# A fourth block product by a second Strassen level in the second layer, two more units done so, and a new order of VectorE's additions

## The chip, the cores and the metric

The kernel runs on one core of a Trainium2 chip, as one launch. The core's engines each work through a queue of their own in order: TensorE (PE in the profile, with its weight loads as PEld), VectorE (DVE), ScalarE (ACT) and GpSimd (POOL). SyncE (SP) issues most of the DMAs; GpSimd issues those that add what they carry to their destination. TensorE writes to PSUM, which has eight banks of 128 partitions by 512 float32 elements here; VectorE or ScalarE must read a bank before it is written anew. The metric is the time of one execution in microseconds (us), as the device reports it.

## What is computed

```python
# q, k, v: (4, 8, 768, 64); w_in: (512, 2048); w_out: (2048, 512); all float32
for t in range(S):                        # retention: a recurrent state per batch and head
    state = gamma * state + einsum('bhd,bhe->bhde', k[:, :, t], v[:, :, t])
    y[:, :, t] = scale * einsum('bhd,bhde->bhe', q[:, :, t], state)
x = y.transpose(0, 2, 1, 3).reshape(B * S, H * D)     # (3072, 512)
h = x @ w_in
out = maximum(0.01 * h, h) @ w_out                    # leaky ReLU between two layers
```

## The kernel before

The 768 time steps are cut into six chunks of 128 steps, each with 512 tokens (4 batches). The 2048 hidden columns are cut into four units of 512. For a chunk and a unit the first layer is a 512 x 512 product with 512 tokens, then the leaky ReLU, then the second layer, whose result is added to the chunk's output `o` (four blocks of 128 x 2 x 256, 2048 elements per partition). Both are done by the Winograd form of Strassen's algorithm: seven block products M1 to M7 instead of eight, on sums and differences of the blocks.

Chunks 0 and 1 are worked in a first part that the change does not touch in its behaviour. Chunks 2 to 5 are worked in the loop at L1445: 16 steps n = 0 to 15, with chunk c = 2 + n // 4 and unit u = n % 4. A step does the second layer of (c, u), while the first layer of the following step n + 1 is done in two groups between its parts:

- `inner_steps` (L1339) is the first layer, by two Strassen levels: the outer products' operands are split again, so that a matmul is 128 x 128 by 128 columns. Group 0 has four of the outer products (28 matmuls, each of two instructions), group 1 the other three (21 matmuls). They use banks 0 to 3. Of the seven inner products, ScalarE copies the results of five out of PSUM, and VectorE adds the last two (M3 once, M7 twice, L1362 to L1365) to what is there. Bank 1 is free after VectorE's M3 addition.
- `outer` (L1374) adds the inner results to the hidden blocks `g`, two additions after group 0 and five after group 1, and gives ScalarE the leaky ReLU of each.
- `differences` (L629) makes the four operands that the second layer needs beside `g`. VectorE does it at the start of a step, ahead of the evacuation of group 0.
- `output` (L741) is the second layer as seven whole products of eight matmul instructions (128 x 128 by 256 columns) each. Steps 0 to 3 and step 15 use it.
- Steps 4 to 14 use `trunk` (L1290) instead: M1, M5, M6 and later M7 as whole products in banks A = 5, C = 7, B = 4, and the remaining three products by a second level in `leaf_steps` (L1255), which are seven inner products of three matmuls each, in banks 6, 7, 2 and 5. Their moving sums are made by GpSimd (`leaf_sums`, L1242, four operations of 384 elements). Their weights are kept in DRAM (`leaf_kept`), written once per unit in steps 0 to 3 from sums that VectorE makes (`sums_of_rows`), and loaded again for every step (`load_rows`, three DMAs of 448 KB).
- `trunk_taken` (L1321) adds banks A and C to `o`, in a chunk's first unit by copies of ScalarE. M6's bank is added inside `trunk`. `leaf_results_taken` (L1279) adds the leaf results to `o`: after units 0 to 2 by a DMA with `accum_op=add` that GpSimd issues, after unit 3 by VectorE, three additions of 512 elements, each stored to the output.
- `sums_of_x` makes the second-level sums of the next chunk's x: in unit 2 those of group 0, in unit 3 those of group 1, which are wanted by group 1 of the same step.
- In units 0 and 1 of chunks 2 to 4 a step also has a *visit* (`joint_visit`, L414) between group 0 and `trunk`: the retention of two batches of the next chunk, in banks 0, 7, 1 and 2. Its first 16 instructions write banks 0 and 7, the next ones bank 1 and 2. VectorE reads all four at L468. Behind the trunk's products follow the scores of the next two batches (`scores_of_pair`, L358) with their masks and state sums on VectorE.

The order of all instructions is the order in which the program writes them; the schedule is manual, and waits come only from data and from buffers in use. In a step by leaves without a visit, before, VectorE has: four differences, three evacuations of group 0, two additions of `outer`, the sums of x where there are some, then M6's addition to `o`, then A's and C's, three evacuations of group 1, five additions of `outer`, M7's addition, three evacuations of the leaves.

All additions of the kernel stand at one line each in the profile, since they go through helpers: L612 (`plus`) and L615 (`minus`).

Of the kernel before, what the change touches and what calls it, by code (L numbers as in the profile page):

```python
# [22 lines left out]
def kernel(  # L23
# [334 lines left out]
    def scores_of_pair(c, b, banks=None, mid=None):  # L358
# [28 lines left out]
        for j in range(2):  # L387
            am = work.tile([128, 2, HP // 2, 2, C // 2], FP32, tag=f"am{j}", name=f"am{j}_{c}_{b}")
            nc.vector.tensor_tensor(
                out=am.rearrange("p b m i t -> p (b m i) t"),  # L390
                in0=at[j].rearrange("p b m i t -> p (b m i) t"),
                in1=mask[:, 0].unsqueeze(1).to_broadcast([128, 2 * HP, C // 2]), op=ALU.mult)
            weights.append(am)
# [7 lines left out]
        if not last:  # L401
            state_of[p] = halves_of_states.pop(0)
            plus(state_of[p], mid, sums[1])
        mid_of[p] = old, mid
# [206 lines left out]
    def plus(out, a, b):  # L611
        nc.vector.tensor_tensor(out=out, in0=a, in1=b, op=ALU.add)  # L612

    def minus(out, a, b):
        nc.vector.tensor_tensor(out=out, in0=a, in1=b, op=ALU.subtract)  # L615
# [13 lines left out]
    def differences(x, t, last=True):  # L629

        minus(t[:, 0], x[:, 1], x[:, 0])
        minus(t[:, 1], x[:, 3], t[:, 0])
        minus(t[:, 2], x[:, 2], t[:, 1])
        if last:
            last_difference(x)

    def last_difference(x):
        minus(x[:, 1], x[:, 3], x[:, 1])
# [169 lines left out]
    last_three = {}  # L808
# [9 lines left out]
    def new_g(c, u):  # L818
# [3 lines left out]
        last_three[c, u] = both[:, 2:5]  # L822
# [361 lines left out]
    leaf_kept = [dram.tile([128, 3, 7, C], FP32, name=f"leaf_kept_{u}") for u in range(NU)]  # L1184
# [3 lines left out]

    def leaf_rooms():

        free = [flat_of(unit(k)[:, 2:5]) for k in (1, 3, 5)]
        spare = [x2_place[0][:, 21 * C :], streamed_flat[0][:, 21 * C :]]
        more = [spare[i // 2][:, ds(i % 2 * 3 * C, 3 * C)] for i in range(4)]
        return free, spare, [x.rearrange("p (q n) -> p q n", q=3) for x in more]

    def rows_of(u):

        if u < NU - 1:
            return [((0, 3, 1), unit(2 * u + 1)[:, 2:5])]
        return [((0, 3, 2), units[2 * u + 1][1]), ((1, 2, 1), last_s4)]  # L1200

    def sums_of_rows(u):

        free, _, more = leaf_rooms()
        if u == NU - 1:
            more = more[0:2] + [x[:, 7 * C : 10 * C].rearrange("p (q n) -> p q n", q=3)
                                for x in free[0:2]]
        bases = []
        for at, blocks in rows_of(u):
            which = slice(*at)  # L1210
            a11, a21, a12, a22 = (blocks[:, :, k, ts(m, C)] for k in range(2) for m in range(2))
            r = [x[:, which] for x in more]
            plus(r[0], a21, a22)
            minus(r[1], r[0], a11)
            minus(r[2], a12, r[1])
            minus(r[3], a11, a21)
            bases.append((which, blocks))

        def keep():
            for which, blocks in bases:  # L1220
# [4 lines left out]
            for j, r in enumerate(more):  # L1225
                nc.sync.dma_start(out=leaf_kept[u][:, :, 3 + j], in_=r)
        return keep

    def load_rows(n):

        free, spare, _ = leaf_rooms()
        leaf_weights[:] = [x[:, 0 : 7 * C].rearrange("p (j n) -> p j n", j=7)
                           for x in (free[0], free[1], spare[1])]
        for to, kept_rows in zip(leaf_weights, (leaf_kept[at_of(n)[1]][:, i] for i in range(3))):
            nc.sync.dma_start(out=to, in_=kept_rows)

    leaf_weights = []

    def by_leaves(n):
        return n >= NU and n < N2 - 1  # L1240

    def leaf_sums(n):  # L1242

        free, spare, _ = leaf_rooms()
        made = [x.rearrange("p (q n) -> p q n", q=3)
                for x in (free[0][:, 7 * C : 10 * C], free[1][:, 7 * C : 10 * C],
                          spare[0][:, 0 : 3 * C])]
        three = last_three[at_of(n)]
        b11, b12, b21, b22 = (three[:, :, k, ts(h, C)] for k in range(2) for h in range(2))
        for out, a, b in ((made[0], b12, b11), (made[1], b22, made[0]), (made[2], b21, made[1]),  # L1250
                          (b12, b22, b12)):
            nc.gpsimd.tensor_tensor(out=out, in0=a, in1=b, op=ALU.subtract)
        return [b11, b21, *made, b22, b12]

    def leaf_steps(n, moving):  # L1255

        ps = [bank[i][:, 0 : 3 * C].rearrange("p (i n) -> p i n", i=3) for i in (6, 7, 2, 5)]
        results = leaf_results()
        for m, q, j, s in INNER:
            for i in range(3):  # L1260
                nc.tensor.matmul(ps[q][:, i], lhsT=leaf_weights[i][:, j], rhs=moving[s][:, i],  # L1261
# [14 lines left out]
    def leaf_results():  # L1276
        return flat_of(unit(5)[:, 2:5]).rearrange("p (i q n) -> p i q n", i=3, q=4)

    def leaf_results_taken(c, o, final):  # L1279

        results = leaf_results()
        if not final:
# [7 lines left out]
    def trunk(c, o, part, first, final):  # L1290
# [3 lines left out]
        for m, x, sa, rhs, start in (("M1", "A", 0, g[:, 0], True), ("M5", "C", 4, gd[:, 0], True),  # L1294
# [14 lines left out]
            elif m == "M7":  # L1309
# [7 lines left out]
                if final:  # L1317
                    nc.sync.dma_start(out=out[c, 3], in_=o[:, 3])
# [292 lines left out]
```

## Time and profile before

| | us |
|---|---|
| three runs | 633.33, 634.01, 635.36 (median 634.01) |
| the profiled execution, whole | 633.81 |
| its span, first to last instruction | 632.1 |
| busy in the span: TensorE, weight loads | 624.7, 570.5 |
| VectorE, ScalarE, GpSimd | 498.1, 283.5, 81.4 |
| step 6 (chunk 3, unit 2), start to start of the next | 22.54 |
| DMA with addition into `o`, issue to landing, median of nine | 9.2 |

The granted clock of TensorE is 1.000 over the span. The page's busy times are sums over an engine's instructions; the chain that ended last is followed back from the last instruction, at each step to what released it. Timelines list an engine's instructions in order of time: start, length, engine, line, operation, output and input, how many, and in brackets how long the engine had been idle and what released it. Where one line stands for several instructions, the length is that of all of them.

Steps start where group 0 of the next step's first layer starts on TensorE: step 2 at 305.15 us, step 3 at 328.18, step 4 at 351.21, step 5 at 378.19, step 6 at 405.25, step 7 at 427.79, step 8 at 450.33, step 9 at 477.32, step 13 at 571.01, step 14 at 593.55, step 15 at 616.09.

### The profile page before, as it was taken

How to read it: one execution, taken by the hardware profiler on the slowest of the kernel's cores; microseconds unless marked ns; L12 is line 12 of the kernel's file. 1: busy time of each engine (PE TensorE's matmuls, PEld its weight loads, DVE VectorE, ACT ScalarE, POOL GpSimd, SP SyncE). 2: the span in 40 equal slices, each digit the busy share in tenths (PEclk: the TensorE clock that was granted, in tenths of full speed). 3: DMA queues.
4: the chain of work that ended last, by engine and by line, in shares of the span. 5: the costliest groups of instructions: out<-in, count | busy, mean ns of one | idle time of the engine just before them, and what ended most of it. 6: DMA issues, size and time to landing. Idle time of an engine off the chain costs nothing.

```text
span 632.1 us, 15063 instructions
## 1 busy us (share of the span) xinstructions
PE 624.7 (99%) x6284; PEld 570.5 (90%) x6284; DVE 498.1 (79%) x803; ACT 283.5 (45%) x559; POOL 81.4 (13%) x98
## 2 busy tenths in 40 slices
PE   8999999999999999999999999999999999999997
PEld 5888888888888889899999999999998999999996
DVE  5679769889979976668887768799848889866765
ACT  5876646347443114352442452634434424544540
POOL 2000000000011010101000033313033023033200
PEclk9999999999999999999999999999999999999999
DMA  8941325547772998295964888998479579689724
GB/s 330 404 138 34 133 67 208 163 145 226 260 276 81 334 350 289 89 347 168 340 209 157 280 293 250 342 293 260 157 240 306 159 230 278 206 263 271 192 45 116
DMA packets 103219, 141.18 MB, mean 223 GB/s; under 512 B 4328, under 2 KB 82024, under 8 KB 103152
## 3 DMA queue, kind: packets, MB, share of 16 engines
q1 hardware_dynamic: 101552, 132.53, 63.3%
q0 software_dynamic: 1296, 7.08, 5.6%
q8 instruction: 49, 0.80, 0.5%
q10 hardware_dynamic: 304, 0.62, 0.3%
q14 instruction: 18, 0.15, 0.1%
HBM read 108.49 MB, written 24.64 MB: 211 GB/s over the span
## 4 chain that ended last, share of the span: by engine, by line
PE 90%; DMA 5%; ACT 2%; DVE 2%; issue 0%; SPq 0%; DVEq 0%; ACTq 0%
PE bank L1348 26%; PE bank L1299 12%; PE bank L668 11%; PE bank L1261 8%; PE C_h L668 4%; PE B_o L668 4%; PE A_h L668 4%; PE A_o L668 4%; PE C_o L668 4%; PE B_h L668 4%; PE D_o L668 2%; PE D_h L668 2%; DMA x_words<-in_weights_dram 1%; DMA wa<-kept 1%; DMA in<-in_kv_dram 1%; PE bank L371 1%
## 5 line engine op out<-in xcount | busy, mean ns | idle before, releaser
L612 DVE TENSOR_TENSOR made<-made,bank 128x512 f32<-128x512 f32 (+1 forms) x96 | 56.1, 617 | 39.9 <-PE bank L1348 35.9
L1348 PEld LDWEIGHTS bank<-x,wb 128*128 128x128 f32 x672 | 77.6, 192 | 1.1 <-ACT bank L1352 0.3
L1348 PE MATMUL bank<-x,wb 128*128 128x128 f32 x672 | 77.9, 275 | 0.1
L612 DVE TENSOR_TENSOR o<-o,bank 128x512 f32<-128x512 f32 (+3 forms) x75 | 55.2, 767 | 24.3 <-ACT bank L782 6.2
L615 DVE TENSOR_TENSOR g<-g 128x512 f32<-128x512 f32 x96 | 64.1, 688 | 5.3 <-ACT g L1390 0.6
L1348 PE MATMUL bank<-x,wa 128*128 128x128 f32 x512 | 67.6, 275 | 0.0
L1299 PE MATMUL bank<-g,w 128*128 128x256 f32 x288 | 66.1, 382 | 0.7 <-DVE x L468 0.7
L1348 PEld LDWEIGHTS bank<-x,wa 128*128 128x128 f32 x512 | 62.8, 192 | 0.3
L1299 PEld LDWEIGHTS bank<-g,w 128*128 128x128 f32 x288 | 53.2, 190 | 8.0 <-DVE x L468 1.1
L1348 PE MATMUL bank<-t,wa 128*128 128x128 f32 x384 | 53.4, 275 | 0.1
L1348 PEld LDWEIGHTS bank<-t,wa 128*128 128x128 f32 x384 | 48.0, 192 | 0.3 <-DMA wa<-kept 0.3
L612 DVE TENSOR_TENSOR g<-made 128x512 f32<-128x512 f32 x64 | 44.0, 709 | 3.0
L1352 ACT COPY bank<-bank 128x512 f32<-128x512 f32 (+1 forms) x32 | 16.6, 520 | 60.1 <-PE bank L1348 59.8
L1390 ACT ACTIVATE g<-g 128x512 f32<-128x512 f32 x64 | 38.5, 631 | 8.2 <-DVE g L612 8.2
L668 PE MATMUL bank<-g,w 128*128 128x256 f32 x168 | 38.0, 382 | 0.0
L668 PEld LDWEIGHTS bank<-g,w 128*128 128x128 f32 x168 | 31.3, 190 | 4.2
L668 PE MATMUL bank<-g,last 128*128 128x256 f32 (+1 forms) x148 | 32.6, 375 | 0.0
L668 PEld LDWEIGHTS bank<-g,last 128*128 128x128 f32 x148 | 27.0, 190 | 3.9 <-DVE g L615 0.4
L1261 PE MATMUL bank<-g,w 128*128 128x128 f32 x176 | 26.8, 275 | 0.0
L668 PE MATMUL A_h<-x,w 128*128 128x256 f32 x112 | 26.6, 380 | 0.0
L1303 ACT COPY bank<-bank 128x512 f32<-128x512 f32 x11 | 6.3, 570 | 41.1 <-PE bank L1299 41.1
L1283 POOL DMA_DIRECT2D o<-w x9 | 8.1, 903 | 125.2 <-DVE g L615 65.6
(255 smaller groups left out, 1234.8 us busy)
## 6 DMA issues: line engine op xcount, KB each, us to landing
wa<-kept SPq DMA_DIRECT2D x16, 1344.0 KB, 9.4
raw<-in_weights_dram SPq DMA_DIRECT2D x31, 512.0 KB, 4.4
wb<-kept SPq DMA_DIRECT2D x16, 896.0 KB, 5.5
w<-leaf_kept SPq DMA_DIRECT2D x22, 448.0 KB, 4.6
wa<-kept SPq DMA_DIRECT2D x16, 448.0 KB, 6.1
wb<-kept SPq DMA_DIRECT2D x16, 448.0 KB, 6.3
o<-w POOLq DMA_DIRECT2D x9, 768.0 KB, 9.2
out_dram<-o SPq DMA_DIRECT2D x23, 256.0 KB, 2.5
```

Source lines behind the costliest of these rows:

```text
L371: nc.tensor.matmul(at[j][ts(h, 64), n, m, i], lhsT=x[ts(j, 64), 1, a, ts(h, 64)], rhs=x[ts(j, 64), 0, a, ts(h, 64)], start=(n == 0 and a = ...
L612: nc.vector.tensor_tensor(out=out, in0=a, in1=b, op=ALU.add)
L615: nc.vector.tensor_tensor(out=out, in0=a, in1=b, op=ALU.subtract)
L668: nc.tensor.matmul(to, lhsT=block(w, sa)[:, k, ts(i, 128)], rhs=rhs[:, k, a:z], start=(first and (i == 0 or split) and n == 0 and k == 0), ...
L1261: nc.tensor.matmul(ps[q][:, i], lhsT=leaf_weights[i][:, j], rhs=moving[s][:, i], start=(i == 0 and m in ("M1", "M5", "M4")), stop=True, sk ...
L1283: nc.gpsimd.dma_start(out=o[:, 0:3].rearrange("p i k n -> p (i k n)"), in_=results.rearrange("p i q n -> p (i q n)"), accum_op=ALU.add)
L1299: nc.tensor.matmul(ps[x][:, i, :], lhsT=block(2 * u + 1, sa)[:, k, ts(i, 128)], rhs=rhs[:, k, :], start=(start and i == 0 and k == 0), sto ...
L1303: nc.scalar.copy(out=ps["B"], in_=ps["A"])
L1348: nc.tensor.matmul(ps[q][:, i], lhsT=w[:, j, i], rhs=part_of(moving[i], s), start=(i == 0 and m in ("M1", "M5", "M4")), stop=True, skip_gr ...
L1352: nc.scalar.copy(out=ps[3], in_=ps[0])
L1390: nc.scalar.activation(g[:, i], g[:, i], AF.Prelu, alpha=0.01)
```

## The change

The fourth product, M7, goes into the leaves as well: `trunk` keeps M1, M5 and M6, and `leaf_steps` does seven inner products of four matmuls. Steps 2 and 3 are done by `trunk` and leaves too, with weights that stay on the chip: their sums are made by GpSimd (four operations of 512 elements in step 1, twelve smaller ones in step 3). VectorE's weight sums for units 0 and 1 are eight operations each (four of 128 and four of 384 elements) instead of four.

After the leaves VectorE adds the result of M7 to another one (512 elements); then the 2048 results go to `o` by the accumulating DMA after units 0 to 2, and by one addition of VectorE at a chunk's end and in step 14. The stores of the output follow that.

In steps without a visit, A's addition stands right behind M1, C's behind M5 with `outer`'s two additions after it, and M6's behind M6, except in unit 2, where it is behind `outer`'s five. In visiting steps the visit with its loads stands ahead of `outer`'s two additions, and GpSimd's leaf sums in step 9 wait for the differences of x. In visiting steps by leaves the scores use banks 1, 6, 2 and 3, and the second mask comes behind the state sums. In step 14 the differences for step 15 stand ahead of the last three inner products of the leaves. The diff, cut to its core:

```diff
     def scores_of_pair(c, b, banks=None, mid=None, second_mask_last=False):
...
+        masks(range(1 if second_mask_last else 2))
...
+        if second_mask_last:
+            masks((1,))
...
+    ON_CHIP = range(2, NU)
...
     def by_leaves(n):
-        return n >= NU and n < N2 - 1
+        return ON_CHIP[0] <= n < N2 - 1
...
     def load_rows(n):
-        for to, kept_rows in zip(leaf_weights, (leaf_kept[at_of(n)[1]][:, i] for i in range(3))):
-            nc.sync.dma_start(out=to, in_=kept_rows)
+        for i in range(4):
+            to = free[(1, 3)[i // 2]][:, ds(i % 2 * 7 * C, 7 * C)]
+            to = to.rearrange("p (j n) -> p j n", j=7)
+            nc.sync.dma_start(out=to, in_=leaf_kept[at_of(n)[1]][:, i])
...
     def leaf_steps(n, moving):
-            for i in range(3):
-                nc.tensor.matmul(ps[q][:, i], lhsT=leaf_weights[i][:, j], rhs=moving[s][:, i],
+            for i, to in enumerate(TARGETS):
+                nc.tensor.matmul(ps[q][:, to], lhsT=leaf_weights[i][j], rhs=moving[s][:, i],
...
-    def leaf_results_taken(c, o, final):
-        results = leaf_results()
-        if not final:
-            nc.gpsimd.dma_start(out=o[:, 0:3].rearrange("p i k n -> p (i k n)"),
-                                in_=results.rearrange("p i q n -> p (i q n)"), accum_op=ALU.add)
-            return
-        for i in range(3):
-            plus(o[:, i], o[:, i], results[:, i].rearrange("p (k h) n -> p k (h n)", k=2))
-            nc.sync.dma_start(out=out[c, i], in_=o[:, i])
+    def leaf_results_taken(n, o, by_dma):
+        results = leaf_results(n)
+        plus(results[:, 2], results[:, 2], results[:, 3])
+        flat = results.rearrange("p i q n -> p (i q n)")
+        o = o.rearrange("p i k n -> p (i k n)")
+        if by_dma:
+            nc.gpsimd.dma_start(out=o, in_=flat, accum_op=ALU.add)
+        else:
+            plus(o, o, flat)
...
+    def trunk_taken(o, first, part):
+        def to(n):
+            return room[part].unsqueeze(1).to_broadcast([128, n, 2, N])
+        if part == "A":
+            if first:
+                nc.scalar.copy(out=o[:, 0], in_=room["A"])
+            else:
+                plus(o[:, 0], o[:, 0], room["A"])
+        elif part == "C":
...
+                plus(o[:, 1:4:2], o[:, 1:4:2], to(2))
...
+        else:
+            plus(o[:, 1:4], o[:, 1:4], to(3))
...
         if visiting:
+            if u == 0:
+                xs[c + 1] = new_x(c + 1)
             joint_visit(c + 1, 2 * u)
-            if by_leaves(n):
+            if leaves:
                 load_rows(n)
+            outer(n + 1, 0)
+            if u == 1:
+                behind = differences(*xs[c + 1])
...
+        if leaves and not visiting:
+            products(steps, 1)
+            trunk_taken(os[c], u == 0, "A")
+            if more and u == NU - 1:
+                sums_of_x(c + 1, 1)
+            products(steps, 1)
+            trunk_taken(os[c], u == 0, "C")
+            outer(n + 1, 0)
+            if c + 1 < NC and u == 2:
+                sums_of_x(c + 1, 0)
+            products(steps, 1)
+            if u != 2:
+                trunk_taken(os[c], u == 0, "B")
         else:
-            products(steps, 1)
+            products(steps, 3)
...
+            if scores_next and leaves:
+                scores_of_pair(*scores_next, [bank[i] for i in (1, 6, 2, 3)],
+                               second_mask_last=True)
...
+        if n in (0, 1):
+            keep.append(sums_of_rows(n))
+        if n in (1, 3):
+            keep.append(sums_of_rows({1: 2, 3: 3}[n], nc.gpsimd))
...
+            if leaves and not visiting and u == 2:
+                trunk_taken(os[c], False, "B")
+        if leaves:
+            leaf = leaf_steps(n, moving)
+            last_one = n + 2 == N2
+            for count, ready in ((1, 1), (1, 1), (2, 2)) if last_one else ((4, 3), (1, 1)):
+                products(leaf, count)
                 for _ in range(ready):
                     later.pop(0)()
-            products(leaves, 8)
-            leaf_results_taken(c, os[c], u == NU - 1)
+            if last_one:
+                differences(*gs[n + 1][1:])
+            products(leaf, 8)
+            leaf_results_taken(n, os[c], u < NU - 1 and not last_one)
+            if u == NU - 1:
+                for i in range(4):
+                    nc.sync.dma_start(out=out[c, i], in_=os[c][:, i])
```

## The prediction

> **What bounds it now.** I read the shares of the engines first, then the chain that ended last in order of time, then the timelines of VectorE, GpSimd and TensorE, step by step.
>
> ```profile
> PE 624.7 (99%) x6284; PEld 570.5 (90%) x6284; DVE 498.1 (79%) x803; ACT 283.5 (45%) x559; POOL 81.4 (13%) x98
> ...
> PE 90%; DMA 5%; ACT 2%; DVE 2%; issue 0%; SPq 0%; DVEq 0%; ACTq 0%
> ```
>
> TensorE has work in 99% of the span, so matmul time removed is time saved as long as no new wait opens. VectorE's 79% is the average; between 526 and 548 us it is busy 20.1 of 22. The chain shows what one step (chunk 3, unit 2; I call it step 6, with steps 0 to 15 for four chunks of four units) costs:
>
> ```profile
> 405.25 6.25 PE bank L1348 x56
> 411.50 5.18 PE bank L1299 x24
> 416.68 4.69 PE bank L1348 x42
> 421.37 1.73 PE bank L1299 x8
> 423.10 4.69 PE bank L1261 x42
> ```
>
> Each line is start, length, instructions: first layer group 0; outer products M1, M5, M6; first layer group 1; the fourth product M7 whole; three products by leaves. They stand end to end: nothing but TensorE sets the length, 22.54 us.
>
> **What TensorE saves.** The new step has 5.18 for M1, M5, M6 and four products by leaves. These are 56 instructions of 128 columns, as many as first layer group 0 has: 6.25. So 1.73 + 4.69 = 6.42 becomes 6.25, 0.17 less, in 11 steps (4 to 14): 1.9 us. Steps 2 and 3 (units 2 and 3 of chunk 2) have seven whole products today, 6.91 + 5.18 = 12.09; afterwards 5.18 + 6.25 = 11.43, so 2 x 0.66 = 1.3. Step 9 has one stall of 0.7 us, where TensorE waits for VectorE's read of a visit's bank; the change puts those reads ahead of two additions and holds GpSimd's sums back, so it goes. In all **-3.9 us**.
>
> **What VectorE gets.** In a step by leaves: evacuations of 512 instead of 384 elements, 3 x (0.68 - 0.55) = 0.4 us, and a new addition of two results, 0.69. At the end of chunks 2 to 4 one addition of 2048 elements, estimated 2.3 (0.69 for 512 and 1.21 for 1024 make 1.04 ns an element), in place of 1.9 today. All M1, M5, M6 additions together stay at 3072 elements. The question is where these stand in its queue, which is in order.
>
> **Part 1: the wait for the accumulating DMA.** After units 0 to 2 GpSimd adds the leaf results to `o` by a DMA. Today VectorE's first addition to `o` comes 12 us into the next step. The change puts the addition of M1's bank (A) right behind M1, which ends 8.0 us into a step (6.25 + 1.73). What is queued behind it: C's addition, two additions of the first layer, the sums of x for the next chunk, and evacuations. When the DMA lands:
>
> ```profile
> 595.26 0.89 POOL L1283 DMA_DIRECT2D o<-w  x1 [16.42 <-DVE g L615]
> ...
> 605.81 2.42 DVE L612 TENSOR_TENSOR o<-o,bank 128x512 f32<-128x512 f32 x3 [3.09 <-DMA o<-w]
> ...
> o<-w POOLq DMA_DIRECT2D x9, 768.0 KB, 9.2
> ```
>
> This is step 14, begun at 593.55: issued at 1.7, landed 10.4 later, 12.1 us into the step; VectorE, with nothing else to do, waited 3.09 us for it. The nine landings take 7.3, 10.1, 9.6, 8.2, 9.4, 8.7, 9.2, 10.4 and, alone at the end, 5.8 us. The six in the steps that the change reorders (6, 7, 10, 11, 13, 14) have a mean of 9.6. Afterwards the DMA moves 1024 KB, and 448 KB more of leaf weights are loaded beside it. Bounds: 5.8 below; above, the part beyond the issue (9.6 - 0.9) times 4/3, 12.5. I take 9.6, the mean of the nearest rows. It is issued 0.6 after the new addition (as today after the last evacuation), which ends at 1.4 + 0.7: landing at 2.1 + 0.6 + 9.6 = 12.3, not 8.0.
>
> [...]
>
> Step 6 then, VectorE: A 13.0, C (1024, 1.21) 14.2, two additions 15.6, eight sums of x (3.25) 18.9, three evacuations of group 1 (1.62) 20.5, five additions 23.8, M6's bank (1536, est. 1.75) 25.5, three leaf evacuations 27.6, result addition 28.3: 5.9 into step 7, where 2.75 would do. ScalarE's fourth leaky waits for the fifth addition, and the copy behind it ends at 25.6 where TensorE wants it at 25.05: 0.6. Step 7: the DMA lands at 5.9 + 0.6 + 9.6 = 16.1; A 16.8; the sums of x that TensorE wants at 12.1 for the second product of group 1 (now 12.7) come at 17.4: 4.7; the third waits 0.45 more. Sum **5.8** for steps 6 and 7, and the same for steps 10 and 11. Step 3 has one such wait behind it (unit 2 of chunk 2 adds by DMA too): landing 13.0, A 13.7, and its sums of x run beside GpSimd's 12 new operations. Beside GpSimd such a sum takes 1.25 to 1.36 (rows at 431 to 436) instead of 0.55: ready at 14.9 and 17.4, TensorE loses 2.9 + 1.85 = **4.7**.
>
> **Part 2: the chunk's end against the visit.** In steps 4 and 8 TensorE goes from the first layer into a visit, whose 17th instruction overwrites bank 1, once VectorE has evacuated it.
>
> ```profile
> 453.30 2.81 DVE L615 TENSOR_TENSOR g<-g 128x512 f32<-128x512 f32 x4
> 456.03 1.88 DVE L612 TENSOR_TENSOR made<-made,bank 128x512 f32<-128x512 f32 x3
> 456.51 0.46 PE L446 MATMUL bank<-am,v 64*64 64x64 f32 x16
> 456.79 0.67 PE L429 MATMUL bank<-qk,states 64*64 64x64 f32 x32
> ```
>
> The first evacuation ends at 456.7, TensorE goes on at 456.79, 6.5 into the step: no slack. Afterwards, with VectorE on time: leaf evacuations 1.4, results 2.1, the whole chunk 4.4, four differences (2.85) 7.2, evacuation 7.9: 1.4 late. With part 1's delay the leaf evacuations end at 2.25: 2.3 late, twice: **4.6**.
>
> **Part 3: the last step.** Step 14 puts the four differences for step 15 ahead of three leaf evacuations. Step 15's M5 writes bank 5 2.6 us in, and the last of these reads it. VectorE even on time: additions to 20.6, M6's 22.4, differences 25.2, evacuations 27.3, against 25.0: 2.3. With A waiting, 27.85: **2.9**. Today it ends at 617.1, 1.0 in.
>
> **At nothing, and their cover.** `outer` behind the visit: its two additions are wanted 10 us later. The second mask behind the state sums: bank 6 is wanted only by the leaves, one group later; bank 3, now 0.6 earlier, ends as M1's copy wants it. Eight weight sums instead of four in steps 0 and 1: 1.1 us against 2.1 and 1.2 of idle VectorE. GpSimd's sums for unit 2, 4 x 1.3, overlap VectorE's in step 1 and cost it some 2 us; 1.3 and 0.5 of idle time follow before anything is wanted. Leaf sums of 512 (1.0 to 1.3 for 384, so 1.3 to 1.7) end at 12, wanted at 17. SP: 11 issues of kept weights instead of 6 in steps 0 and 1 (some 0.6 each) put wa's load in step 2 up to 3 us back; it lands by 20, wanted at 22.4. The fourth row's load, 448 KB, has 16 us. wa's 9.1 ends 1 us ahead of need in the visiting steps: 0, or 1 each.
>
> **Sum.** -3.9 + 5.8 + 5.8 + 4.7 + 4.6 + 2.9 = **+19.9**. The profiled execution took 633.8 (span 632.1 and 1.7 around it), the median is 634.0: 653.7. With 12.5 for the DMA the same working gives 11.5 for a pair of steps and some +40: 673.
>
> **Rivals.** (1) *The DMA lands in time*, below 5.9 us after its issue. For it: the 5.8 row. Against: it was alone; eight rows exceed it by 1.5 or more. Then parts 2 and 3 remain at 2 x 1.4 + 2.3 = 5.1, and 633.8 - 3.9 + 5.1 = 635.0. (2) *Faster: VectorE's queue is on time everywhere.* The mechanism is the length of its queue at a chunk's end: if the 2048-element addition and the new one go 1.4 us faster than my 3.0 (both read SBUF alone, and no row here has that size) and the DMA lands in time, the visits don't wait, and 629.9 plus at most the last step's 2.3 remain. It turns at 7.9 against 6.5. For it: 20.1 of 22 us leaves room on average. Against: 0.633 us for every 512 from SBUF at 451 us. (3) *Longer yet*: landing near 12.5, above 670. (4) The saving fails because four products by leaves stall on their own: unlikely, as group 0 runs the same pattern without a gap; it would take back at most 3.2.
>
> **Numbers.** Forecast 653.7, with its own range of 636 to 670: 0.70. Rival 1: 0.10. Rival 2: 0.14. Above 670: 0.06. A measurement here can tell 0.3%, 1.9 us, from no change. So faster 0.14, same 0.10, slower 0.76. The range leaves out rival 2 and the tail: 632 to 670.
>
> **What would show it.** Part 1: VectorE idle 3 us or more for `o<-w` in steps 3, 6, 7, 10, 11, 13 and 14, and TensorE idle ahead of group 1 in steps 3, 7 and 11. Part 2: TensorE waiting for `made` at a visit's start in steps 4 and 8. Part 3: a wait of 2 us in step 15's M5. TensorE's busy time should be 3.2 lower. Landings below 7 us, or A's addition not waiting, make the prediction wrong.

## The result and the profile after

| | before | after |
|---|---|---|
| median of four runs, us | 634.0 (633.33 to 635.36) | 656.98 (655.98 to 657.29) |
| profiled execution, span, us | 633.8, 632.1 | 656.8, 655.0 |
| granted clock over the span | 1.000 | 0.986 |
| TensorE waits in the loop that the change brings, us | - | 16.6 |

After takes 1.0357 times as long, 95% interval 1.0336 to 1.0378: 23 us slower. The forecast was 653.7. The page of after, first the busy times, then the granted clock in 40 slices (each digit in tenths, a slice is 16.4 us), then the engines' shares of the chain that ended last:

```profile
PE 631.6 (96%) x6398; PEld 579.2 (88%) x6398; DVE 513.9 (78%) x799; ACT 294.4 (45%) x564; POOL 112.9 (17%) x122
...
PEclk9999999999999999999999999997999998999998
...
PE 69%; DVE 16%; DMA 10%; issue 2%; ACT 2%; POOL 0%; SPq 0%; DVEq 0%; POOLq 0%; ACTq 0%
```

TensorE's share of the chain fell from 90% to 69%, and VectorE and the DMA took its place. One thing was not foreseen: TensorE's busy time is 6.9 us higher, though its matmuls should take 3.2 less. The waits of after, by what TensorE waited for (total, times, longest):

```profile
PE bank L1382 <- DVE x L622: 8.3, 5, 3.4
PE bank L1382 <- ACT bank L1386: 3.9, 2, 2.3
PE bank L436 <- DVE made L619: 2.5, 3, 1.2
PE bank L674 <- DVE w L619: 2.0, 1, 2.0
```

L1382 is the first layer, L436 the visit, L674 the last step. These are the places that the prediction named. How one comes about is seen in the timelines of GpSimd, VectorE and TensorE in step 7, which begins at 433.00:

```profile
440.56 0.89 POOL L1327 DMA_DIRECT2D o<-w  x1 [19.56 <-DVE w L619]
...
442.79 1.88 DVE L619 TENSOR_TENSOR made<-made,bank 128x512 f32<-128x512 f32 x3
449.37 0.69 DVE L619 TENSOR_TENSOR o<-o,bank 128x512 f32<-128x512 f32 x1 [4.70 <-DMA o<-w]
449.97 0.55 DVE L622 TENSOR_TENSOR x<-x 128x384 f32<-128x384 f32 x1
...
446.35 0.83 PE L1382 MATMUL bank<-x,wb 128*128 128x128 f32 x6
450.58 6.99 PE L1382 MATMUL bank<-x,wb 128*128 128x128 f32 x36 [3.40 <-DVE x L622]
```

GpSimd issues the accumulating DMA 7.6 us into the step. VectorE idles 4.70 us for it, adds A, and only then makes the sums of x that TensorE has been waiting for since 447.2. The last line holds the surprise: 36 matmul instructions take 6.99 us, where at the rate of the group's usual 4.69 for 42 they take 4.02. The granted clock says why. The windows below give for each stretch of after its length, the busy time of TensorE (with instructions), of its weight loads, VectorE, ScalarE and GpSimd, then the granted clock:

```profile
446.04:449.45 3.41, 1.14 (x9) 0.90 (x7) 0.08 (x1) 0.46 (x1) 2.19 (x2) 1.00 0.98 227
449.45:452.86 3.41, 2.28 (x10) 2.28 (x11) 3.34 (x6) 0.48 (x1) 0.00 (x0) 0.50 1.04 374
452.86:456.27 3.41, 3.41 (x18) 3.41 (x17) 3.31 (x4) 1.12 (x3) 0.00 (x0) 0.50 0.02 7
456.27:459.69 3.42, 3.42 (x33) 3.42 (x32) 2.64 (x6) 1.18 (x3) 0.00 (x0) 1.00 0.19 32
```

After a window with 1.14 us of work in 3.41, TensorE runs for two windows at half clock: 18 instructions in 3.41 us instead of 33. There are five such windows in the loop, one in step 3, two in step 7, one each in steps 11 and 15. By the granted 0.50, a window of half clock costs half of the time in it that TensorE works: 1.7 us in four of them and 1.14 in the first of the two above, together 8.0.

Where the 23 us are, by the steps' lengths in the two traces (matmuls as the prediction has them; windows of half clock by the last paragraph):

| step | longer by | waits | half clock | matmuls | rest |
|---|---|---|---|---|---|
| 2 | -0.65 | | | -0.66 | 0.0 |
| 3 | 4.87 | 2.62 + 0.79 | 1.7 | -0.66 | 0.4 |
| 4 | 1.45 | 1.18 | | -0.17 | 0.4 |
| 7 | 8.12 | 1.65 + 3.40 | 2.8 | -0.17 | 0.4 |
| 8 | 1.23 | 1.18 | | -0.17 | 0.2 |
| 9 | -0.85 | -0.7 (gone) | | -0.17 | 0.0 |
| 11 | 6.06 | 2.27 + 1.27 + 0.25 | 1.7 | -0.17 | 0.7 |
| 15 | 4.0 | 2.0 | 1.7 | | 0.3 |
| 5, 6, 10, 12 to 14, and before step 2 | -1.3 | | | -1.0 | -0.3 |
| all | 22.9 | 16.6 - 0.7 | 8.0 | -3.2 | 2.2 |

### The profile page after: what moved, and what is told of

Read it like the earlier page. It is cut to its first block, busy times and chain, and to the rows that moved or that the text cites. A ratio compares the mean times of both kernels' runs of the same rounds, so it can differ in the third digit from the quotient of the medians.

```text
span 655.0 us, 15350 instructions
## 1 busy us (share of the span) xinstructions
PE 631.6 (96%) x6398; PEld 579.2 (88%) x6398; DVE 513.9 (78%) x799; ACT 294.4 (45%) x564; POOL 112.9 (17%) x122
## 4 chain that ended last, share of the span: by engine, by line
PE 69%; DVE 16%; DMA 10%; issue 2%; ACT 2%; POOL 0%; SPq 0%; DVEq 0%; POOLq 0%; ACTq 0%
PE bank L1382 15%; DMA o<-w 9%; PE bank L1305 8%; PE bank L674 7%; PE bank L1338 5%; DVE o L619 4%; PE C_h L674 4%; PE B_o L674 4%; PE A_h L674 4%; PE C_o L674 4%; PE A_o L674 4%; PE B_h L674 4%; DVE w L619 3%; DVE made L619 3%; DVE g L619 3%
## 5 line engine op out<-in xcount | busy, mean ns | idle before, releaser
L1382 PE MATMUL bank<-x,wb 128*128 128x128 f32 x672 | 83.9, 285 | 8.3 <-DVE x L622 8.3
L1382 PEld LDWEIGHTS bank<-x,wb 128*128 128x128 f32 x672 | 82.1, 201 | 10.4 <-DVE x L622 9.3
L619 DVE TENSOR_TENSOR o<-o,bank 128x512 f32<-128x512 f32 (+4 forms) x58 | 53.8, 949 | 45.8 <-DMA o<-w 31.0
L1382 PE MATMUL bank<-x,wa 128*128 128x128 f32 x512 | 68.9, 277 | 4.0 <-ACT bank L1386 3.9
L1382 PEld LDWEIGHTS bank<-x,wa 128*128 128x128 f32 x512 | 63.3, 193 | 4.7 <-ACT bank L1386 4.3
L1382 PE MATMUL bank<-t,wa 128*128 128x128 f32 x384 | 54.4, 279 | 0.0
L1338 PE MATMUL bank<-g,w 128*128 128x256 f32 x240 | 53.9, 381 | 0.0
L1338 PEld LDWEIGHTS bank<-g,w 128*128 128x128 f32 x240 | 44.8, 190 | 6.0
L1382 PEld LDWEIGHTS bank<-t,wa 128*128 128x128 f32 x384 | 49.2, 196 | 0.0
L1305 PE MATMUL bank<-g,w 128*128 128x128 f32 x400 | 48.7, 275 | 0.0
L1305 PEld LDWEIGHTS bank<-g,w 128*128 128x128 f32 x400 | 46.7, 192 | 0.0
L1386 ACT COPY bank<-bank 128x512 f32<-128x512 f32 (+1 forms) x32 | 16.6, 519 | 59.6 <-PE bank L1382 55.9
L1316 ACT COPY w<-bank 128x512 f32<-128x512 f32 x52 | 30.2, 583 | 11.9 <-PE bank L1305 11.9
L619 DVE TENSOR_TENSOR w<-w,bank 128x512 f32<-128x512 f32 x39 | 25.1, 683 | 7.9 <-PE bank L1305 7.0
L674 PE MATMUL A_h<-x,w 128*128 128x256 f32 x112 | 26.6, 380 | 0.0
L163 POOL TENSOR_TENSOR in<-in,dec 128x512 f32<-128x512 f32 x2 | 2.3, 1150 | 139.9 <-DMA raw<-in_weights_dram 139.9
```

Source lines behind the costliest of these rows:

```text
L163: engine.tensor_tensor(out=v, in0=v, in1=gk[c].unsqueeze(2).to_broadcast([128, H, D]), op=ALU.mult)
L619: return nc.vector.tensor_tensor(out=out, in0=a, in1=b, op=ALU.add)
L674: nc.tensor.matmul(to, lhsT=block(w, sa)[:, k, ts(i, 128)], rhs=rhs[:, k, a:z], start=(first and (i == 0 or split) and n == 0 and k == 0), ...
L1305: nc.tensor.matmul(ps[q][:, to], lhsT=leaf_weights[i][j], rhs=moving[s][:, i], start=(i == 0 and m in ("M1", "M5", "M4")), stop=True, skip ...
L1316: nc.scalar.copy(out=results[:, :, {"M5": 3, "M4": 2, "M6": 1, "M2": 0}[m]], in_=ps[q])
L1338: nc.tensor.matmul(ps[x][:, i, :], lhsT=block(2 * u + 1, sa)[:, k, ts(i, 128)], rhs=rhs[:, k, :], start=(start and i == 0 and k == 0), sto ...
```

## The experiments

The theory to test: it is the order on VectorE and nothing in the amount of work, that is, A's and C's additions ahead of what TensorE needs (part 1), the chunk's end ahead of the visit (part 2), step 14's differences (part 3), and half clock behind the longer waits. The rivals: VectorE simply has too much work; the clock falls for another reason. The twelve kernels, in the order in which they were tried, each beside runs of before (633.6 to 634.1 us) on the same chip:

| kernel | us | ratio to before, 95% |
|---|---|---|
| late additions | 640.8 | 1.008 to 1.013 |
| no accumulating DMA | 648.6 | 1.021 to 1.028 |
| idle matmuls in the waits | 654.8 | 1.030 to 1.034 |
| before, with A early | 636.3 | 1.002 to 1.006 |
| late, step 14's order | 640.4 | 1.008 to 1.013 |
| late, chunk's end deferred | 650.2 | 1.022 to 1.031 |
| late from step 3, both of these | 648.3 | 1.022 to 1.025 |
| DMA of three rows | 649.8 | 1.024 to 1.029 |
| late, ends mended | 635.0 | 1.001 to 1.003 |
| ends mended, three more moves | 635.2 | 1.001 to 1.004 |
| ends mended, additions early | 653.8 | 1.030 to 1.033 |
| ends mended, split differences | 632.9 | 0.997 to 0.999 |

**Late additions.** A's and C's additions go behind the sums of x, in steps without a visit:

```diff
         if leaves and not visiting:
-            products(steps, 1)
-            trunk_taken(os[c], u == 0, "A")
+            products(steps, 3)
             if more and u == NU - 1:
                 sums_of_x(c + 1, 1)
-            products(steps, 1)
-            trunk_taken(os[c], u == 0, "C")
             outer(n + 1, 0)
             if c + 1 < NC and u == 2:
                 sums_of_x(c + 1, 0)
-            products(steps, 1)
+            trunk_taken(os[c], u == 0, "A")
+            trunk_taken(os[c], u == 0, "C")
```

> The changed kernel with the additions of A and C to `o` moved behind the sums of x and the first layer's two additions, in the steps without a visit; nothing else is moved. Theory (VectorE stands in its queue behind the accumulating DMA, and TensorE runs at half clock after its waits): the waits of steps 3, 7 and 11 go, 2.62 + 0.79 + 1.65 + 3.40 + 2.27 + 1.27 + 0.25 = 12.25 us, and the half clock behind them, 3.0 + 1.85 + 1.7 = 6.55 us: 657.0 - 18.8 = 638.2 us, between 636 and 642, with the visits' 1.2 to 1.4 us in steps 4 and 8 and the 2 us of step 15 left. Rival (VectorE simply has too much work in these steps): the order doesn't matter, and 650 us or more stay.

640.8 us: 16 of the 23 us are gone. Steps 3, 7 and 11 take 22.46, 22.62 and 22.38 us (27.90, 30.66, 28.60 in after), with the same instructions. The rival falls. The waits that are left, in the view by releaser:

```profile
PE bank L436 <- DVE made L619: 5.1, 3, 2.5
PE bank L674 <- DVE w L619: 1.8, 1, 1.8
PE bank L1305 <- DVE o L619: 1.3, 1, 1.3
```

The visits of steps 4 and 8 wait 2.46 us each, not the 1.2 to 1.4 that I expected. Step 2, which has no DMA behind it, got 1.27 us for A's bank.

**No accumulating DMA.** VectorE adds the results in every unit; the early places stay.

```diff
-            leaf_results_taken(n, os[c], u < NU - 1 and not last_one)
+            leaf_results_taken(n, os[c], False)
```

> The changed kernel without the accumulating DMA: VectorE adds the leaf results to `o` in every unit, one addition of 2048 elements, 2.29 us, in 9 more steps; the early places of A and C stay. Theory (the DMA's landing is what is late): although VectorE gets 9 x 2.29 = 20.6 us more work, the time falls, because nothing waits for a transfer; the new additions stand ahead of the visits in steps 5 and 9 too, so 4 visits wait 1.4 to 2 us, and step 15 its 2 us and the half clock behind it: 632.1 - 3.9 + 1.7 + 6 + 4 = 640 us, between 636 and 648. Rival (VectorE has too much work): slower than the changed kernel, up to 657 + 20 = 677 us.

VectorE is busy 546.1 us instead of 513.9, and the kernel is 8.4 us faster than after. So waiting for the landing costs more than the 32 us of additional work on VectorE; but 648.6 is above the 640 that I worked out and just outside its range, since the additions now make VectorE late themselves:

```profile
PE bank L1382 <- DVE x L622: 7.0, 4, 2.1
PE bank L436 <- DVE made L619: 5.7, 5, 2.0
```

I had counted the visits' 5.7 (as 6) and nothing for the sums of x, which still stand behind A.

**Idle matmuls in the waits.** They fill the first part of the four long waits (the diff shows steps 3 and 7; steps 11 and 15 have theirs in the same way):

```diff
-            inner(n + 1, 1)
+            rest = inner_steps(n + 1, 1)
+            if n in (3, 7):
+                products(rest, 1)
+                for _ in range({3: 6, 7: 9}[n]):
+                    fill(6)
+            products(rest, 8)
```

> The changed kernel with idle matmuls of 512 bf16 columns ahead of the four waiting ones: 6 in step 3, 9 in step 7, 6 in step 11, 4 in step 15 (some 0.2 us each), into a bank that nobody uses then. They give TensorE something to do in the first part of each wait and shorten the idle stretch to about 1.3 us; what TensorE waits for comes no earlier. Theory (an idle stretch of 2 us or more puts TensorE to half clock): the waits' ends stay where they are and the half clock behind them goes, 3.0 + 1.85 + 1.7 + 1.8 = 8.4 us, less what later waits take back: 649 us, between 647 and 653, and a granted clock of 1.00 throughout. Rival (the clock falls for a reason other than idleness, or the waits alone are the loss): 656 to 658 us, and a clock of 0.50 in the same places.

In step 7 it does what it should. TensorE's timeline there (L707 are the idle ones):

```profile
448.90 2.11 PE L707 MATMUL bank<-mask 128*128 128x512 bf16 x9
452.41 0.94 PE L1382 MATMUL bank<-x,wb 128*128 128x128 f32 x6 [1.40 <-DVE x L622]
453.59 3.62 PE L1382 MATMUL bank<-x,wb 128*128 128x128 f32 x30 [0.25 <-DVE x L622]
```

The 36 instructions run at full clock behind a window with 1.04 us of idle time (2.27 in after), and the step takes 28.46 us instead of 30.66. The clock went with the idle time here, then, and not with the place. Yet in all only 2.2 us of the expected 8 came (1.030 to 1.034 times before, where after has 1.034 to 1.038): what TensorE gained it partly lost at the next wait. With step 3 shorter by 0.64, the visit of step 4 waits 1.94 us instead of 1.18 and has half clock behind it (30.68 us, 28.43 in after); in step 11 the first wait is gone and the second is 2.48 us, with half clock again. Four of the five windows of half clock went, the one of step 11 stayed, and one came in step 4. My sum failed, as far as step 4 shows, since TensorE at half clock gives VectorE time to catch up (1.18 us of wait in step 4 with half clock in step 3, 1.94 without): this loss and the next wait are not to be added.

**Before, with A early.** The kernel before, A's addition behind M1, and unit 3's sums of x behind that:

```diff
+            if early:
+                part = gs.pop(n)
+                steps = trunk(c, os[c], part, u == 0, u == NU - 1)
+                products(steps, 1)
+                plus(os[c][:, 0], os[c][:, 0], room["A"])
+            if u == NU - 1:
+                sums_of_x(c + 1, 1)
             outer(n + 1, 0)
```

> The kernel before with one thing of the change alone: in units 2 and 3 without a visit, and in units 1 to 3 of the last chunk, A's addition to `o` stands behind M1 and ahead of the first layer's two additions and of the sums of x (those of unit 3 came at the step's start before). The instructions are those of before, no more and no other. Theory: the DMA lands about 12 us into the step, A ends at 12.6, VectorE ends the step some 3 us later than in before, the next DMA lands at about 14.6, and the sums wanted at 12.1 are 3 to 4 us late in steps 7 and 11, with 2 to 3 us of half clock behind each wait: 634 + 2 x 5.5 = 645 us, between 641 and 651. Rival (it is the added operations that count): within 1 us of before.

Expected 645, measured 636.3. The mechanism is there, but not the price. GpSimd's and VectorE's timelines in its step 7, which begins at 428.76:

```profile
431.29 0.88 POOL L1283 DMA_DIRECT2D o<-w  x1 [18.63 <-DVE g L615]
...
438.54 0.69 DVE L612 TENSOR_TENSOR o<-o,bank 128x512 f32<-128x512 f32 x1 [2.05 <-DMA o<-w]
```

The DMA is issued 2.5 us into the step, against 7.6 in after, and lands 7.2 later, against 8.7: the sums of x are ready when TensorE wants them. Of the 2.3 us that this kernel lost, 1.31 lie in step 6, where M7 waits for VectorE's additions to `o`, and 0.69 in step 15. In after the same order meets a longer list (VectorE's M6 addition behind `outer`'s five, one more result addition, larger evacuations) and a DMA that lands later. The early place needs that lateness to hurt, and the lateness is passed from step to step, since a late VectorE issues the next DMA late. That the longer list makes the difference is argued from the two traces; no run lengthens it alone.

**DMA of three rows.** The size by itself, in after's own order; the fourth row of units 0 to 2 stays out of the output:

```diff
-            nc.gpsimd.dma_start(out=o, in_=flat, accum_op=ALU.add)
+            nc.gpsimd.dma_start(out=o[:, 0 : 12 * C], in_=flat[:, 0 : 12 * C], accum_op=ALU.add)
```

> The changed kernel, in its own order, but the accumulating DMA moves only the first three of the four rows of the results (768 KB instead of 1024): a quarter of the leaf sums of units 0 to 2 is left out of the output. It tells how much of the wait is the DMA's size. If the time to landing goes with the size beyond the issue, it falls from 9.7 on the mean to 7.5, some 2 us in each of the six steps with a wait, and the waits of 11.5 us in steps 3, 7 and 11 mostly go: 642 to 648 us. If other traffic and a fixed part make up most of it (the landings of the 768 KB form in the kernel before had a mean of 8.7), 1 us less in each: 650 to 655 us.

The nine landings have a mean of 8.6 us (9.7 in after): a quarter of the bytes is worth 1.1 us of some 9. But the time falls by 7.2, to 649.8, since the lateness is carried on, as the waits suggest: in steps 7 and 11 the waits ahead of ScalarE's copy fall from 1.65 and 2.27 to 0.39 and 0.55, and step 7 has one window of half clock instead of two.

**Step 14's order**, on the late kernel:

```diff
+            products(leaf, 8)
             if last_one:
                 differences(*gs[n + 1][1:])
-            products(leaf, 8)
```

> The kernel with late additions of A and C (640.8 us), and in step 14 the four differences for the last step behind the leaf evacuations, ahead of the results' additions, as the kernel before had them behind the evacuations. Theory: bank 5 is then read 2.9 us earlier, and the first difference, which M5 needs as well, ends at about 23.4 us into the step, ahead of 25.0: the wait of 1.85 us in step 15 goes, and the half clock behind it (3.4 us at half speed, 1.7): 640.8 - 3.5 = 637.3 us, between 636 and 638.5. Rival (the differences are what is late, wherever they stand): 640 to 642.

In the trace the edit does its work: the wait of 1.85 us becomes 0.52, the half clock in step 15 goes, and steps 14 and 15 together take 35.5 us instead of 38.5. The medians, 640.4 and 640.8, don't show it: the executions of the two kernels scatter over 3 us, and the profiled one lost 1.3 us in steps 6 and 9. So the trace shows the 3 us, the times do not.

**The chunk's end deferred**, behind the next visit, with the stores; and both edits, late only from step 3 on:

```diff
+            if u == NU - 1:
+                ended.append(taken)
+            else:
+                taken()
...
             joint_visit(c + 1, 2 * u)
+            while ended:
+                ended.pop()()
```

> The kernel with late additions of A and C (640.8 us), and at the chunk's end the results' addition, the addition of 2048 elements and the stores behind the next step's visit, or behind its first layer group 0 where it has no visit. Theory: the 0.69 + 2.29 us stand ahead of the evacuation that the visit waits for; without them the two waits of 2.46 us in steps 4 and 8 go, and the half clock that one of them brings (1.7): 640.8 - 6.6 = 634.2 us, between 633 and 636. Rival (VectorE's total is the limit, so the deferred 3 us only come due later in the same step): 638 us or more, with a new wait behind the visit.

> Both of the edits before together, and the additions of A and C late only from step 3 on, since step 2 has no DMA behind it and got a wait of 1.27 us for bank 5 by the late order. Theory (order alone made the changed kernel slow): no wait above 1 us is left, the granted clock is 1.00, and what remains is the saving in matmuls: 640.8 - 3.5 - 6.6 - 1.3 = 629.4 us, or 634.1 - 3.9 = 630.2 from the other side: between 628.5 and 632, ahead of both kernels. Rival (four products by leaves, or the added work, cost something of their own): 634 us or more.

Both failed: 650.2 and 648.3. The visits don't wait any more, but a wait that I hadn't seen took the place. ScalarE's and TensorE's timelines in step 4 of the first of the two:

```profile
369.88 0.59 ACT L1352 COPY o<-bank 128x512 f32<-128x512 f32 x1 [7.72 <-DMA out_dram<-o]
...
371.74 0.51 ACT L1386 COPY bank<-bank 128x384 f32<-128x384 f32 x1
...
372.31 0.94 PE L1382 MATMUL bank<-x,wb 128*128 128x128 f32 x6 [3.07 <-ACT bank L1386]
```

`o` has one buffer for these chunks: ScalarE's first copy into the next chunk's `o` waits 7.72 us for the deferred stores, and the copies for the first layer stand behind it. Steps 4, 8 and 12 of this kernel have 10.0 us of such waits, the longest 5.3 in step 12. The order of the change, which adds and stores ahead of the visit, has a reason.

**Ends mended.** Only the differences change places with the first layer's evacuation in steps 4 and 8; addition and stores stay (late additions and step 14's order as above):

```diff
-            differences(*gs[n][1:])
+            behind_it = visiting and u == 0 and n > 0
+            if not behind_it:
+                differences(*gs[n][1:])
...
             products(begun, 7)
+            if behind_it:
+                differences(*gs[n][1:])
```

> The kernel with late additions of A and C and step 14's differences behind the evacuations (640.4 us), and in steps 4 and 8 the four differences (2.8 us) behind the evacuation that the visit waits for, where they stood ahead of it; the addition of 2048 elements and the stores stay where the changed kernel has them, so the one buffer of `o` comes free as early as there. Theory: the waits of 2.46 and 2.00 to 2.46 us in steps 4 and 8 go, and the 1.7 us of half clock behind one of them; TensorE wants the first difference 3.5 us after the evacuation, when it has been made: 640.4 - 4.5 to 4.9 - 1.7 = 634.0 us by this working, and 640.8 - 3.5 - 4.9 - 1.7 = 630.7 if step 15's edit shows its full gain as the profile has it: between 630 and 635. Rival (the waits only move, as they did when the additions at the chunk's end were deferred): 639 us or more.

635.0 us, 1.002 times before, and no window of half clock in the loop. The amount of work is that of after, 799 instructions on VectorE and 6398 on TensorE:

```profile
PE 623.4 (98%) x6398; PEld 571.8 (90%) x6398; DVE 529.3 (84%) x799; ACT 294.6 (46%) x564; POOL 117.2 (18%) x122
```

All three parts were order. What is left against 630.2, before less its 3.9, lies in step 2 (23.75 us, expected 22.37), step 4 (27.96, 26.81), step 8 (27.50, 26.83), step 9 and step 15.

**Three more moves**, on the kernel with its ends mended: the first difference alone ahead of the visit's reads, step 14's first difference ahead of the last evacuation, and step 2's sums of x at its start.

```diff
+            if n == 2:
+                sums_of_x(c + 1, 0)
...
             if behind_it:
-                differences(*gs[n][1:])
+                x, t = gs[n][1:]
+                minus(t[:, 0], x[:, 1], x[:, 0])
...
             joint_visit(c + 1, 2 * u)
+            if behind_it:
+                other_differences(*part[1:])
```

> The kernel with late additions of A and C and mended ends (635.0 us), with three more moves on VectorE: in steps 4 and 8 only the first difference stands ahead of the visit's reads of its banks and the other three behind them; in step 2 the sums of x stand at the step's start, ahead of the differences, where GpSimd does not work yet (beside it, two of them took 2.60 us instead of 0.62); in step 14 the first difference stands ahead of the last evacuation. Theory: what the last kernel lost against the forecast of matmuls alone, 1.4 us in step 2, 1.15 and 0.7 in steps 4 and 8 and 0.7 in step 15, 3.9 us in all, was VectorE's order in these places: 631.5 us, between 630.5 and 633.5, ahead of both kernels. Rival (VectorE's amount of work in the steps with a visit and beside GpSimd is the limit): 634 us or more.

Step 2's move changes the computation: the sums of the next chunk's x overwrite those that step 2's own first layer still reads. It also costs: TensorE waits for the sums in the middle of that layer, in its timeline

```profile
307.54 0.49 PE L1387 MATMUL bank<-x,wa 128*128 128x128 f32 x2 [1.57 <-DVE x L622]
...
308.86 4.53 PE L1387 MATMUL bank<-x,wa 128*128 128x128 f32 x24 [0.83 <-DVE x L622]
```

and runs at half clock behind it; step 2 takes 26.90 us. In all it takes 635.2 us, where I expected 631.5. Steps 4 and 8 got shorter by 0.83 and 0.69, of 1.15 and 0.7 expected. So the same without step 2's move:

> The kernel of the last trial without its move in step 2: the sums of x stand where they stood, behind the first layer, and the split differences of steps 4, 8 and 14 stay. In the last trial step 2 took 26.90 us instead of 23.75, since its first layer then waited 1.57 and 0.83 us for sums written early into a room that it still reads, with half clock behind it; steps 4 and 8 took 0.83 and 0.69 us less than in the kernel of 635.0 us. Theory (what was lost at the visits was the order alone): 635.2 - 3.15 = 632.0 us, between 631 and 633.3, ahead of before by 0.1 to 0.4%. Rival (the gains in steps 4 and 8 came only from TensorE being later by step 2's wait, which gave VectorE time): 634 to 635.5.

632.9 us, 0.998 times before (0.9969 to 0.9992): ahead of both kernels, though less far than the 632.0 of the working. Of before's 634 less 3.9, some 2.8 us are still missing. Steps 2, 4 and 9 hold 1.5, 1.0 and 0.6 of it by their lengths. Step 8 keeps its gain (26.81 us), but step 4 keeps only 0.15 (27.81): its wait of 0.42 us behind the visit is gone, yet TensorE now idles 0.59 us later in the step, where the profile names nothing that it waits for. Step 2's is the 1.27 us for A's bank:

```profile
PE bank L1310 <- DVE o L619: 1.3, 1, 1.3
```

**Ends mended, additions early.** After's order of A and C with everything else mended: the price of part 1 alone.

> The changed kernel with its early additions of A and C, but with the ends of the chunks and step 14 mended as in the kernel of 635.0 us: the two differ in the place of A's and C's additions alone. If the parts of the loss add up, the visits' 1.18 + 1.18 us and step 15's 2.0 + 1.7 us go from 657.0: 650.9 us, between 648 and 653, and part 1 alone is worth 16 us. If a late visit gives VectorE time that it needs afterwards, the waits of steps 7 and 11 grow instead: 653 us or more.

653.8 against 635.0 us, 18.8 apart. From step 1's start to the end, where alone the two differ in order, the profiled executions are 16.2 apart (368.5 and 352.3), as the parts added up would have it; the first part of the program took 2.1 us longer in the profile of this kernel. Of these, 1.8 arise in a window of half clock there, which no other profile has. TensorE's time in it and in the window ahead of it (columns as above):

```profile
4.85:8.26 3.41, 2.26 (x50) 1.72 (x52) 0.96 (x1) 0.12 (x1) 0.00 (x0) 1.00 0.99 357
8.26:11.68 3.42, 3.42 (x40) 1.76 (x34) 1.30 (x2) 0.95 (x3) 2.05 (x2) 0.50 1.03 408
```

So part 1 is worth 16.2 us by the traces. The time of 653.8 lies outside the 648 to 653 that I expected, but the waits of steps 7 and 11 did not grow, as the other account had it: they sum to 4.9 and 4.0 us, against 5.05 and 3.79 in after. Whether the other three executions, all within 1 us of this one, lost the rest in the same place is not on record.

## Why the prediction was right, and where it was not

- **The saving in matmuls, 3.9.** Right. Steps without a wait take 22.38 us instead of 22.54, in after and in all variants, and step 9's stall is gone. TensorE's busy time was not 3.2 lower, as the prediction said it would be, since half clock made it longer; without half clock it is 1.3 lower in the kernel with its ends mended (623.4) and 2.5 lower in the last one (622.2).
- **Part 1, the landing of 9.6 us.** Right on the mean, 9.7, but not for the single ones. The DMAs issued in steps 6 and 10 take 11.4 and 12.0 and land 14.1 and 14.7 us into the step, where the prediction had 12.3. Those issued in steps 7 and 11 take 8.7 and 8.2, but are issued 7.6 and 8.2 us in instead of 6.5: they land at 16.3 and 16.4, where the prediction had 16.1, by two errors that cancel. All nine take 8.2 to 12.0. TensorE's waits are where the prediction put them, but the sizes are not all right: ScalarE's copy came 1.65 and 2.27 us late instead of 0.6, the sums of x 3.40 and 1.52 instead of 5.15. In the pair of steps 6 and 7 they sum to 5.05 us, in steps 10 and 11 to 3.79 (5.8 predicted for each), in step 3 to 3.41 (4.7).
- **Part 2, the visits, 2 x 2.3.** 1.18 each in after. TensorE itself was late by then, at half clock in steps 3 and 7, and VectorE had, it seems, caught up. Where those windows are absent and the additions late, the wait is 2.46.
- **Part 3, the last step, 2.9.** 2.0 measured, and 1.7 of half clock.
- **The missing term.** The prediction's waits, 5.8 + 5.8 + 4.7 + 4.6 + 2.9 = 23.8, measured 16.6: too large by 7. It had no term for the granted clock: 8.0, too small by that. The two nearly cancel, and they seem to be linked: the visits waited 1.18 us each with half clock ahead of them, 2.46 without. The total fell 3 us short of the median by luck as much as by working; the mechanism of each part is what held.
- **The rivals.** Rival 1 (the DMA in time) and rival 2 (VectorE on time everywhere) did not come: VectorE idled 31.0 us for the landing in six steps of after. The seventh that the prediction named is step 6, where it idled 6.42 us; the view puts this down to ScalarE, but the DMA issued at 413.27 landed 11.4 us later, 0.1 us ahead of the addition. Rival 3 (above 670) did not come either. Rival 4 falls too: four products by leaves show no stall of their own, and with another order the change is ahead of before. The waits by releaser, and VectorE's addition of A in step 6:

```profile
DVE o L619 <- DMA o<-w: 31.0, 6, 7.0
...
424.77 0.69 DVE L619 TENSOR_TENSOR o<-o,bank 128x512 f32<-128x512 f32 x1 [6.42 <-ACT made L1390]
```

What stays open: 2.2 us of after spread over the steps with waits, most of the 2.8 us by which the last kernel misses the full saving, and why the executions with the chunk's end deferred scatter over 7 us (647.0 to 654.3).

## What to carry to other kernels

VectorE worked its queue in order here, so a cheap instruction that waits for a transfer is priced by what stands behind it: in step 7 of after, A's addition of 0.69 us waited 4.70 us for the DMA, and TensorE lost 3.40 us to the sums of x behind it. Put what the busiest engine needs ahead of such an instruction, and look before any deferral for the buffer that the deferred work keeps occupied: with the chunk's end deferred, ScalarE waited 7.72 us for `o`. Lateness is passed on from step to step while it also sets when the next transfer starts, so a term worked out for one step in isolation can be off by several times in either direction: ScalarE's copy, 0.6 us late by the prediction, came 2.27 late in step 11, and the waits for the sums of x there took 1.52 instead of 5.15. And when a change opens waits on TensorE, price the clock behind them as well: the four of 2.0 to 3.40 us in after had half clock behind them, 8.0 us in all.

## What the runs showed of the hardware

**When the clock halves.** Within the profiled execution of after the changes of the granted clock lie on a grid: it falls at 343.65, 449.45, 545.05 and 640.60 us. Three of these four stretches of half clock last 3.41 us, the second 6.82, and their starts are 31.0, 28.0 and 28.0 times 3.41 us apart (296.95 us in all, 87 times 3.413). I divided the traces of after and of seven variants, from 298 us on, into such windows, aligned to a change of the clock in each. Every window of these at full clock in which TensorE idled 1.88 us or more was followed by half clock (16 windows), none with 1.83 or less was (33 windows with 0.87 or more), and of two with 1.85 one was. So in these it is the idle share of a window that tells them apart, 1.85 of 3.41 us or 54%, and not the length of a wait. The late kernel has two waits of 2.46 us, in steps 4 and 8; the first falls into one window, the second is cut by a border:

```profile
356.70:360.11 3.41, 1.53 (x27) 1.27 (x25) 3.27 (x6) 0.00 (x0) 0.10 (x1) 1.00 0.63 231
360.11:363.52 3.41, 2.84 (x106) 2.84 (x109) 1.71 (x3) 0.00 (x0) 0.10 (x1) 0.50 0.26 97
...
459.10:462.51 3.41, 2.73 (x37) 2.47 (x36) 3.27 (x4) 0.92 (x2) 0.10 (x1) 1.00 0.24 85
462.51:465.92 3.41, 1.64 (x110) 1.64 (x112) 2.91 (x5) 0.00 (x0) 0.10 (x1) 1.00 0.61 227
465.92:469.34 3.42, 3.42 (x31) 2.99 (x24) 2.71 (x6) 1.07 (x2) 0.00 (x0) 1.00 0.53 158
```

A window at half clock with 1.13 us of idle time was followed by another, one with 0.57 was not. The limit is not so sharp outside these windows. In the kernel with its ends mended and its additions early, the window at 4.85 us, with 1.15 us of idle time, was followed by half clock (its line stands above). In the kernel before, the last window with work, with 1.93 us of idle time, was not:

```profile
627.01:630.42 3.41, 1.48 (x11) 1.23 (x9) 1.80 (x5) 0.00 (x0) 0.00 (x0) 1.00 0.71 249
630.42:633.83 3.41, 0.00 (x0) 0.00 (x0) 0.00 (x0) 0.00 (x0) 0.00 (x0) 1.00 0.05 14
```

What counts beside idle time is open. A window need not be idle throughout: in the late kernel's first line above, 1.53 us of work in 3.41 did not keep the clock.

**VectorE beside GpSimd.** The same two subtractions of 128 elements, from and to SBUF, took 2.60 us beside GpSimd's leaf sums (314.70 to 320.34) in step 2 of the kernel with its ends mended, and 0.62 at the step's start in the next one, where GpSimd stood still until 313.94. VectorE's timelines, first beside GpSimd, then alone:

```profile
314.86 2.60 DVE L622 TENSOR_TENSOR x<-x,x 128x128 f32<-128x128 f32 x2
```

```profile
307.52 0.62 DVE L622 TENSOR_TENSOR x<-x,x 128x128 f32<-128x128 f32 x2
```

VectorE's busy time is 528.3 us in the late kernel and 513.9 in after, with the same 799 instructions, which fits: in after VectorE idles for the DMA in part of the time in which GpSimd works. For this pair the factor is 4.2; what makes it, the traces do not show.
